# The opening of an attention and two-layer expert kernel: a new order of loads, sums, Newton's chain and weight conversions

## The chip, the cores and the metric

The kernel runs on one core of one Trainium2 chip. The core has TensorE (matrix products and transposes, PE in the profile, its weight loads PEld), VectorE (DVE), ScalarE (ACT), GpSimd (POOL) and SyncE (SP), whose queue issues the transfers between device memory and on-chip memory here. The metric is the time of one execution in microseconds (us) on the device, as a median of several runs.

## The reference, cut to what matters

First comes Nystrom attention over 4 batches of 8 heads, 576 rows and 64 columns per head. The rows are averaged in 32 groups of 18 to landmarks, and an inverse is found by Newton's iteration. Then two gated layers of 2304 tokens follow, 512 wide and 1536 inside.

```
m = 32; scale = 1.0 / np.sqrt(D)
q_lm = q.reshape(B, H, m, S // m, D).mean(axis=3)
k_lm = k.reshape(B, H, m, S // m, D).mean(axis=3)
A, Bm, C = sm(q, k_lm), sm(q_lm, k_lm), sm(q_lm, k)      # sm: softmax of scale * a @ b.T
Z = Bm.T / (norm1(Bm) * norminf(Bm) + 1e-06)
for _ in range(6):
    Z = 2 * Z - Z @ Bm @ Z
x = (A @ Z @ C @ v)                                      # heads side by side: 2304 x 512
x = (silu(x @ w_gate) * (x @ w_val)) @ w_out
out = (sigmoid(x @ w2_gate) * (x @ w2_val)) @ w2_out
```

## The kernel before, in words

A batch `b` is worked on in two groups `g` of four heads; the four heads' 32 landmarks each fill the 128 partitions. The steps of attention are generators:

- `front(b, g)`, word `F`: `lm_steps` for the key, then for the query. The 18 rows of each landmark are summed (`lm`): VectorE does it in one reduction for group (0,0), POOL by halving additions (L127 to L132) for all others. TensorE transposes the sum (`lt`), ScalarE makes the block-diagonal `bdk` or `bdq` from it, and nine transposes `tp` with ScalarE copies make `kq` (kT or qT). Then `cs`, the scores of the landmark queries against all keys, VectorE's maximum `cmx`, ScalarE's exponential `e`; the small matrix `bm` with its exponential `bs` and `rc`, a reciprocal; transposes of `e` (`et`), and the product with v (`cv`, scaled into `bc`, BC in the code). Last come the scores of all queries (`as`) with `amx`, the subtraction and exponential (`sx`).
- `back(b)`, word `B`: `bs` of both groups is divided by its sums, `rr` is made from its largest row and column sums, and Newton's chain runs on the pair [small matrix, C v] side by side (`nw` on TensorE, `rw` on VectorE, five turns and one last that gives UU), then `ut`, the transposed result. `a_steps` normalizes `sx`, transposes it and splits it into a high and a low half (`AH`, two per group); one step of it is given after each Newton turn by `step(ga)`.
- The first layer's weights (`c` is one of six chunks of 256 inner columns) come in as `raw` tiles, three buffers, four transfers of 128 KB each for the four tiles of a chunk, and are converted to float32 words (`convert`: two ScalarE instructions, L329 and L332, two of VectorE, L334 and L338). `wo` tiles, two buffers, hold the output weights. These steps are `wfill`.
- Word `U` (`uw_steps`): the product of `ut` and the converted weights (`pu`), split into two halves `uw`; it starts with a two-column product (`pu<-ident`) that needs neither. Word `G` (`gv1_steps`): gate and value products `pg`, `pv` of `AH` and `uw`. Both need both groups' `AH` and `uw`. Word `O`: the output product `po`. `I` and `J` give conversion steps until a chunk's inputs or outputs are ready.

The words of `first` are given in order, L812 on. A planner lays out each engine's queue from that: it estimates when an instruction can start and prefers what was given first, so the order in a queue is not quite the program's. At run time each queue goes in order. A tile asked for under a tag takes one of its buffers and waits until the readers of the old one are done. All transfers named here go through SP's queue; a transfer that waits for a buffer holds back those behind it. `load_next` asks for a group's input two groups ahead (v one ahead), into four buffers `in` and one `vin`.

The lines that the prediction speaks of: L120 to L152 (landmarks), L157 to L224 (rest of `front`), L226 to L242 (`AH`), L251 to L305 (`back`), L309 (first loads), L318 to L341 (`convert`), L346 (`load_in`), L812 (order).

## Time and profile before

| | us |
|---|---|
| median of 3 runs (867.75 to 869.99) | 869.67 |
| the profiled execution | 868.88 |
| its span, first to last instruction | 867.1 |
| TensorE busy in the span | 839.1 (97%) |
| VectorE busy | 660.2 (76%) |
| ScalarE busy | 474.2 (55%) |
| POOL busy | 58.5 (7%) |

The span in 40 equal slices of 21.7 us, busy share in tenths, with the granted TensorE clock and the DMA engines' share:

```profile
PE   6698999999999999999999999999999999999998
...
DVE  4989886866976987579698667879778985578655
ACT  5687565455752754237257655555647385455431
...
PEclk9899999999999999999999999999999999999999
DMA  8776311022520631006114316244335552232003
```

A digit is a mean over its slice. TensorE is below 9 in the first, second and fourth slice, and its clock in the second. The opening of the attention lies in these slices, up to 87 us; from there on TensorE's digits are 9 up to the last.

### The profile page before, as it was taken

The page shows a single profiled execution, that of the slowest core. Times are in us where ns is not written, and L with a number is a line of the kernel's source. Part 1 is how long each engine was busy: PE and PEld are TensorE (multiplying, and loading weights), DVE is VectorE, ACT ScalarE, POOL GpSimd, SP SyncE. Part 2 cuts the span into 40 slices and gives each one's busy share as a digit, 9 for nine tenths or more (in the row PEclk, how much of TensorE's full clock was granted, in tenths as well). Part 3 has the DMA queues.
Part 4 walks back from the last instruction along what each step waited for, and adds up shares of the span by engine and source line. Part 5 has one row for each costly group of instructions (what it writes and reads, how often), then busy time and mean ns, then how long its engine had stood idle before and what let it go on. Part 6 is the DMA issues. An engine that isn't in the chain of part 4 may idle for free.

```text
span 867.1 us, 15869 instructions
## 1 busy us (share of the span) xinstructions
PE 839.1 (97%) x6172; PEld 695.4 (80%) x6172; DVE 660.2 (76%) x1295; ACT 474.2 (55%) x967; POOL 58.5 (7%) x90
## 2 busy tenths in 40 slices
PE   6698999999999999999999999999999999999998
PEld 4476778898788888888878888888888888888886
DVE  4989886866976987579698667879778985578655
ACT  5687565455752754237257655555647385455431
POOL 4644330000000000000000000000000000000000
PEclk9899999999999999999999999999999999999999
DMA  8776311022520631006114316244335552232003
GB/s 261 200 222 199 110 56 30 2 77 55 161 98 2 195 98 50 1 25 220 49 43 152 122 41 203 87 157 142 125 126 170 166 176 97 68 122 73 5 20 97
DMA packets 41483, 93.31 MB, mean 108 GB/s; under 512 B 5824, under 2 KB 8896, under 8 KB 41408
## 3 DMA queue, kind: packets, MB, share of 16 engines
q1 hardware_dynamic: 40256, 90.72, 33.2%
q10 hardware_dynamic: 1152, 1.57, 0.8%
q8 instruction: 48, 0.79, 0.4%
q14 instruction: 27, 0.22, 0.1%
HBM read 72.88 MB, written 19.40 MB: 106 GB/s over the span
## 4 chain that ended last, share of the span: by engine, by line
PE 87%; DVE 6%; ACT 3%; DMA 2%; issue 1%; SPq 0%; ACTq 0%; DVEq 0%
PE po L65 33%; PE pg L65 21%; PE pv L65 21%; PE pu L65 3%; PE pgr L65 2%; PE pvr L65 2%; DMA raw<-in_moe_w_val_dram 1%; PE tp L148 1%; PE nw L65 1%; PE cs L65 1%; PE as L65 1%; DVE xl L366 1%; ACT cv L329 1%; PE et L198 1%; DVE lm L134 0%
## 5 line engine op out<-in xcount | busy, mean ns | idle before, releaser
L65 PE MATMUL po<-wo,h 128*128 128x512 f32 x432 | 109.9, 391 | 0.0
L65 PEld LDWEIGHTS po<-h,wo 128*128 128x128 f32 x480 | 82.6, 188 | 27.8 <-issue 5.9
L65 PE MATMUL po<-h,wo 128*128 128x512 f32 (+1 forms) x480 | 104.3, 373 | 0.0
L65 PE MATMUL pg<-AH,uw 128*128 128x288 f32 x552 | 94.8, 299 | 1.3 <-ACT uw L365 1.0
L65 PEld LDWEIGHTS po<-wo,h 128*128 128x128 f32 x432 | 80.7, 188 | 17.6
L65 PE MATMUL pv<-AH,uw 128*128 128x288 f32 x552 | 91.7, 296 | 0.5 <-DVE sg L537 0.5
L772 DVE TENSOR_TENSOR oacc<-po,oacc 128x512 f32<-128x512 f32 x90 | 60.0, 682 | 36.2 <-PE po L65 36.1
L65 PEld LDWEIGHTS pg<-AH,uw 128*128 128x128 f32 x552 | 80.1, 188 | 6.4 <-issue 2.5
L65 PEld LDWEIGHTS pv<-AH,uw 128*128 128x128 f32 x552 | 78.9, 188 | 4.0 <-issue 1.7
L329 ACT ACTIVATE cv<-raw 128x512 f32<-128x512 f32 x84 | 56.8, 677 | 31.8 <-DVE st L338 8.9
L334 DVE SCALAR_TENSOR_TENSOR cv<-cv,cv 128x512 uint32<-128x512 uint32 x84 | 57.8, 690 | 1.8 <-ACT cv L332 1.6
L65 PE MATMUL po<-hh,wo 128*128 128x288 f32 x256 | 58.9, 310 | 0.0
L332 ACT ACTIVATE cv<-raw 128x512 uint32<-128x512 uint32 x84 | 55.9, 670 | 2.1 <-DVE wo L366 2.1
L595 DVE TENSOR_TENSOR acc<-po,acc 128x512 f32<-128x512 f32 x64 | 43.3, 685 | 15.6 <-PE po L65 15.4
L540 ACT ACTIVATE sg<-pg 128x288 f32<-128x288 f32 x64 | 26.0, 407 | 46.7 <-PE pg L65 46.4
L65 PE MATMUL pg<-AH,wk 128*128 128x512 f32 x192 | 50.0, 390 | 0.0
L65 PE MATMUL pv<-AH,wk 128*128 128x512 f32 x192 | 49.5, 389 | 0.0
L65 PEld LDWEIGHTS po<-hh,wo 128*128 128x128 f32 x256 | 41.6, 189 | 4.8 <-issue 2.4
L365 ACT CAST h<-h 128x288 fp32r<-128x288 f32 x64 | 27.5, 431 | 29.9 <-DVE h L541 29.9
L366 DVE TENSOR_TENSOR h<-h,h 128x288 fp32r<-128x288 f32 x64 | 29.1, 456 | 17.9 <-ACT h L365 17.6
L65 PEld LDWEIGHTS pv<-AH,wk 128*128 128x128 f32 x192 | 36.0, 188 | 7.5
L65 PEld LDWEIGHTS pg<-AH,wk 128*128 128x128 f32 x192 | 35.7, 188 | 7.4 <-ACT c5g L694 0.2
(206 smaller groups left out, 1759.7 us busy)
## 6 DMA issues: line engine op xcount, KB each, us to landing
raw<-in_moe_w_out_dram SPq DMA_DIRECT2D x36, 512.0 KB, 3.9
raw<-in_moe_w_gate_dram SPq DMA_DIRECT2D x48, 128.0 KB, 3.4
raw<-in_moe_w_val_dram SPq DMA_DIRECT2D x48, 128.0 KB, 3.4
raw<-in_moe_w_gate_dram SPq DMA_DIRECT2D x24, 256.0 KB, 3.0
raw<-in_moe_w_val_dram SPq DMA_DIRECT2D x24, 256.0 KB, 3.7
wkd<-st SPq DMA_DIRECT2D x24, 256.0 KB, 3.2
wtd<-tf SPq DMA_DIRECT2D x12, 512.0 KB, 3.3
st<-wkd SPq DMA_DIRECT2D x24, 256.0 KB, 3.5
```

The lines of the kernel that those rows point to most:

```text
L65: return nc.tensor.matmul(o, l, r, start=start, stop=stop, skip_group_check=True)
L148: nc.tensor.transpose(ps[:, j], flat(src[:, 2 * u:2 * u + 2]), ident)
L198: nc.tensor.transpose(ps[:, j, :], flat(e[:, r // 2, r % 2]), ident)
L329: nc.scalar.activation(t0, hiw.bitcast(F32), AF.Copy, scale=2.0 ** -112)
L332: nc.scalar.activation(u1, low, AF.Copy, scale=0.875 * 2.0 ** -29, bias=0.49)
L334: nc.vector.scalar_tensor_tensor(u1, u0, 3, u1, op0=ALU.logical_shift_left, op1=ALU.bitwise_or)
L365: nc.scalar.copy(hi, x)
L366: nc.vector.tensor_tensor(lo, x, hi.bitcast(F32), op=ALU.subtract)
L540: nc.scalar.activation(sg, pss[0], AF.Silu)
L595: nc.vector.tensor_tensor(sl, ps, sl, op=ALU.add)
L772: nc.vector.tensor_tensor(acc, ps, acc, op=ALU.add)
```

## The change

The first loads are given as k, q of group (0,0), k, q of group (0,1), v(0,0), the first raw weight tile, v(0,1). Two of these tiles stand in `wo` buffers: v(0,1), and the fourth raw tile of chunk 0. The second raw tile is given behind the issue of k(1,0), the third and fourth behind q(1,0). `lm` has two buffers. The key of group (0,1) is summed by VectorE as the first group is, its copy made by VectorE, and its `bdk` has a buffer of its own. In `back`, `bs` is scaled per group, and ScalarE makes `BC` from the unscaled `bs` with the scale as its operand. For batch 0, the steps of `front(0,0)`, `front(0,1)` and `back(0)` are given by hand: up to Newton's end first, then the first weights' conversions, then `as`, `sx` and `a_steps`. `tc.issue_after(x)` puts every instruction given inside the block behind x in x's own engine's queue: one conversion behind `bs` (ScalarE) and `rc` (VectorE) of group (0,0), three behind `BC` and `rr`; the rest of group (0,0) up to `cv` behind the query transpose `lt` of group (0,1) on TensorE.

```diff
     inq = {}
+    mark = {}
     def load_attn(b, which, g):
         if which == "v":
-            t = att.tile([TP, 4, R, D], F32, tag="vin", name=f"vin{b}_{g}", bufs=1)
-            nc.sync.dma_start(t, v[b, 4 * g:4 * g + 4].rearrange("h (p r) d -> p h r d", r=R))
+
+            pool_, tag, bufs = (per, "wo", 2) if (b, g) == (0, 1) else (att, "vin", 1)
+            t = pool_.tile([TP, 4, R, D], F32, tag=tag, name=f"vin{b}_{g}", bufs=bufs)
+            ins = nc.sync.dma_start(t, v[b, 4 * g:4 * g + 4].rearrange("h (p r) d -> p h r d", r=R))
         else:
             t = att.tile([P, L, D], F32, tag="in", name=f"{which}in{b}_{g}", bufs=4)
             src = {"q": q, "k": k}[which]
-            nc.sync.dma_start(t, src[b, 4 * g:4 * g + 4].rearrange("h (t u) d -> (h t) u d", u=L))
+            ins = nc.sync.dma_start(t, src[b, 4 * g:4 * g + 4].rearrange("h (t u) d -> (h t) u d", u=L))
         inq[which, b, g] = t
+        mark[which, b, g] = ins.ins
     NU = L // 2
...
     def load_next(b, g, which):
         i = AORDER.index((b, g)) + (1 if which == "v" else 2)
-        if i < len(AORDER):
+        if i < len(AORDER) and (which, *AORDER[i]) not in inq:
             load_attn(AORDER[i][0], which, AORDER[i][1])
     def step(fill, n=1):
...
         def lm_steps(which):
             src = inq[which, b, g]
-            lm = sm("lm", [P, 2, D], 1)
-
-            if (b, g) > (0, 0):
+            lm = sm("lm", [P, 2, D])
+
+            if (b, g, which) not in ((0, 0, "k"), (0, 0, "q"), (0, 1, "k")):
                 x = sm("ls", [P, NU, D], 1)
                 nc.gpsimd.tensor_tensor(x, src[:, 0:NU], src[:, NU:], op=ALU.add)
                 nc.gpsimd.tensor_tensor(x[:, 0:4], x[:, 0:4], x[:, 4:8], op=ALU.add)
...
                     nc.gpsimd.tensor_tensor(lm[:, w], x[:, 0], x[:, 1], op=ALU.add)
             else:
                 nc.vector.tensor_reduce(lm[:, 0], src.rearrange("p u d -> p d u"), axis=AX.X, op=ALU.add)
-                nc.scalar.copy(lm[:, 1], lm[:, 0])
+                (nc.vector.tensor_copy if g else nc.scalar.copy)(lm[:, 1], lm[:, 0])
             yield
             ps = pst(b, [P, P], "lt", g)
-            nc.tensor.transpose(ps, flat(lm), ident)
-            bdt = sm("bd" + which, [P, 2, P], 1)
+            mark["lt", which, b, g] = nc.tensor.transpose(ps, flat(lm), ident).ins
+
+            bdt = (per.tile([P, 2, P], F32, tag="CL", name="bdk01", bufs=16) if (b, g, which) == (0, 1, "k") else
+                   sm("bd" + which, [P, 2, P], 1))
             for w in range(2):
                 nc.scalar.activation(bdt[:, w], ps, AF.Copy, scale=pmask[:, w:w + 1])
             yield
...
             mm(ps[hs], bdq[:, 0, hs], bdk[:, 0, hs])
         nc.vector.tensor_reduce(bmx, ps, axis=AX.X, op=ALU.max)
         nc.vector.tensor_scalar(bs[:, g], ps, bmx, None, op0=ALU.subtract)
-        nc.scalar.activation(bs[:, g], bs[:, g], AF.Exp, scale=8.0, accum_out=bsm[:, g:g + 1])
+        mark["bs", b, g] = nc.scalar.activation(bs[:, g], bs[:, g], AF.Exp, scale=8.0, accum_out=bsm[:, g:g + 1]).ins
         rc = sm("rc", [P, 1])
         nc.vector.tensor_scalar(rc, csm[:, 0:1], csm[:, 1:2], 1e-9, op0=ALU.add, op1=ALU.add)
-        nc.vector.reciprocal(rc, rc)
+        mark["rc", b, g] = nc.vector.reciprocal(rc, rc).ins
         yield
         eT = sm("eT", [TP, R, P], 1)
         for hf in range(2):
...
         for g in range(2):
             nc.vector.tensor_scalar(bsm[:, g:g + 1], bsm[:, g:g + 1], 1e-9, None, op0=ALU.add)
         nc.vector.reciprocal(bsm, bsm)
-        nc.vector.tensor_tensor(bs, bs, bsm[:, :, None].to_broadcast([P, 2, M]), op=ALU.mult)
-        nc.scalar.copy(BC[:, :, 0:M], bs)
-
-        bmt = sm("bmt", [P, 2, M])
+        for g in range(2):
+            mark["BC", b] = nc.scalar.activation(BC[:, g, 0:M], bs[:, g], AF.Copy, scale=bsm[:, g:g + 1]).ins
+            nc.vector.tensor_scalar(bs[:, g], bs[:, g], bsm[:, g:g + 1], None, op0=ALU.mult)
+
+        nb = sm("nb", [P, 4, M], 1)
+        bmt = nb[:, 0:2]
         nc.vector.transpose(out=flat(bmt), in_=flat(bs))
         nrm = sm("nrm", [P, 2, 2])
         nc.vector.tensor_reduce(nrm[:, 0], bs, axis=AX.X, op=ALU.add)
         nc.vector.tensor_reduce(nrm[:, 1], bmt, axis=AX.X, op=ALU.add)
         yield
-        nb = sm("nb", [P, 4, M], 1)
         nc.vector.tensor_copy(nb, nrm.rearrange("p a b -> p (a b)")[:, :, None].to_broadcast([P, 4, M]))
         nbt = sm("nbt", [P, 4, M], 1)
         nc.vector.transpose(out=flat(nbt), in_=flat(nb))
...
         for g in range(2):
             nc.vector.tensor_scalar(rr[:, g:g + 1], nmax[:, 0, g:g + 1], nmax[:, 1, g:g + 1], 1e-6,
                                     op0=ALU.mult, op1=ALU.add)
-        nc.vector.reciprocal(rr, rr)
+        mark["rr", b] = nc.vector.reciprocal(rr, rr).ins
         yield
...
             RW2 = sm("rw", [P, 2, 96], 2)
             nc.vector.scalar_tensor_tensor(RW2, RW, 2.0, ps, op0=ALU.mult, op1=ALU.subtract)
             RW = RW2
-            step(ga)
+            if b:
+                step(ga)
             yield
         ps = prod(RW)
         UU = flat(sm("rw", [P, 2, 96], 2))[:, 0:P].rearrange("p (g d) -> p g d", g=2)
...
         while ga:
             step(ga)
             yield
-
-    for g in range(2):
-        for x in "kqv" if g == 0 else "kq":
-            load_attn(0, x, g)
     W1 = {}
...
         return per.tile([P, 2, 2 * FC], U32, tag="raw", name="raw", bufs=3)
     def load_in(layer, c, kk):
-        t = raw_tile()
+
+        t = raw_tile() if (layer, c, kk) != (0, 0, 3) else per.tile([P, 2, 2 * FC], U32, tag="wo", name="raw3", bufs=2)
         for j, w in enumerate(((wg1, wv1), (wg2, wv2))[layer]):
             if layer == 0:
...
     KINDS = {"F": front, "B": back, "I": lambda c: weights_to(c, 3), "J": lambda c: weights_to(c, 5),
              "U": uw_steps, "P": uw_steps, "G": gv1_steps, "O": o1_steps}
+    def advance(gen, n):
+        for _ in range(n):
+            next(gen, None)
+
     def emit(word, nw=1):
         gens = [iter(KINDS[t[0]](*map(int, t[1:]))) for t in word.split("+")]
         fill = word[0] in "UPGO"
...
             if fill:
                 step(wfill, nw)
+
+    for g, x in ((0, "k"), (0, "q"), (1, "k"), (1, "q"), (0, "v")):
+        load_attn(0, x, g)
+    load_to(1)
+    load_attn(0, "v", 1)
     wfill.extend(weights(0, c) for c in range(2))
     first = (
-        "F00 F01 B0 I0 F10 U00 G00 F11 J0 O00 B1 I1 U10 G10 J1 F20 O10 U01 G01 "
+        "I0 F10 U00 G00 F11 J0 O00 B1 I1 U10 G10 J1 F20 O10 U01 G01 "
         "F21 U11 B2+F30 O01 G11 F31 U02 O11 G02 B3 U12 O02 G12 U03 O12 G03 U13 O03 G13"
     )
+
+    f0, f1, b0 = front(0, 0), front(0, 1), back(0)
+    advance(f0, 14)
+    with tc.issue_after(mark["k", 1, 0]):
+        load_to(2)
+    with tc.issue_after(mark["q", 1, 0]):
+        load_to(4)
+    advance(f1, 10)
+    with tc.issue_after(mark["lt", "q", 0, 1]):
+        advance(f0, 3)
+    advance(f1, 7)
+    advance(b0, 10)
+    with tc.issue_after(mark["bs", 0, 0]), tc.issue_after(mark["rc", 0, 0]):
+        step(wfill, 3)
+    with tc.issue_after(mark["BC", 0]), tc.issue_after(mark["rr", 0]):
+        step(wfill, 9)
+    for gen in (f0, f1, b0):
+        advance(gen, 99)
     for w in first.split():
         emit(w)
     wfill.append(weights(0, 2))
```

## Rows read from the trace of the kernel before

**Rows 1.** The page, part 4: the chain that ended last, by engine.

```profile
PE 87%; DVE 6%; ACT 3%; DMA 2%; issue 1%; SPq 0%; ACTq 0%; DVEq 0%
```

**Rows 2.** Windows: length, busy time (instructions) of PE, PEld, DVE, ACT, POOL; PEclk, DMA share, GB/s.

```profile
4.76:24.55 19.79, 14.75 (x237) 11.09 (x238) 11.50 (x28) 12.23 (x38) 11.37 (x19) 1.00 0.93 280
24.55:41.73 17.18, 13.29 (x256) 7.92 (x254) 16.15 (x38) 11.75 (x26) 11.46 (x16) 0.86 0.71 188
41.73:50.00 8.27, 6.19 (x154) 3.92 (x155) 7.94 (x20) 7.63 (x18) 0.00 (x0) 0.67 0.70 215
...
50.00:70.00 20.00, 19.83 (x261) 17.34 (x261) 16.57 (x46) 16.67 (x44) 9.15 (x12) 1.00 0.81 229
70.00:90.00 20.00, 16.92 (x211) 11.91 (x211) 19.05 (x41) 13.90 (x33) 9.46 (x12) 1.00 0.66 186
90.00:110.00 20.00, 19.58 (x273) 15.93 (x272) 15.57 (x38) 9.68 (x27) 7.45 (x12) 1.00 0.27 87
```

**Rows 3.** Timeline of VectorE: start us, length, instruction, [idle before <-releaser].

```profile
...
7.74 2.13 DVE L134 TENSOR_REDUCE lm<-qin 128x64 f32<-128x1152 f32 x1 [0.91 <-PE lt L138]
...
13.38 0.94 DVE L170 TENSOR_REDUCE cmx<-cs 128x1 f32<-128x288 f32 x2 [3.51 <-PE cs L65]
...
23.96 0.21 DVE L190 TENSOR_SCALAR rc<-csm 128x1 f32<-128x1 f32 x1
...
24.55 1.21 DVE L254 TENSOR_TENSOR bs<-bs,bsm 128x64 f32<-128x64 f32 x1
...
29.82 0.32 DVE L288 TENSOR_TENSOR rw<-nw,rr 128x192 f32<-128x192 f32 x1
...
40.59 0.27 DVE L299 SCALAR_TENSOR_TENSOR rw<-rw,nw 128x128 f32<-128x128 f32 x1
...
```

**Rows 4.** Timeline of TensorE.

```profile
...
20.56 0.69 PE L65 MATMUL cs<-kq,bdq 128*32 128x288 f32 x8
...
39.46 0.53 PE L65 MATMUL nw<-rw 32*32 32x96 f32 x16 [0.99 <-DVE rw L293]
...
43.35 1.96 PE L65 MATMUL pu<-w,ut 64*32 64x512 f32 x16 [1.95 <-DVE w L338]
...
49.86 0.40 PE L65 MATMUL pg<-AH,uw 128*128 128x288 f32 x1
...
```

**Rows 5.** Timeline of POOL.

```profile
...
10.27 1.40 POOL L127 TENSOR_TENSOR ls<-kin 128x576 f32<-128x576 f32 x1 [8.97 <-DMA kin<-in_k_dram]
...
24.27 1.41 POOL L127 TENSOR_TENSOR ls<-qin 128x576 f32<-128x576 f32 x1
...
```

**Rows 6.** SP's timeline, then the DMA issues of v and q(0,1) with us to landing.

```profile
1.66 0.42 SPq L74 DMA_DIRECT2D vin<-in_v_dram  x1
...
2.83 0.45 SPq L78 DMA_DIRECT2D qin<-in_q_dram  x1
...
vin<-in_v_dram SPq DMA_DIRECT2D x1, 576.0 KB, 7.4
...
qin<-in_q_dram SPq DMA_DIRECT2D x1, 576.0 KB, 9.5
```

**Rows 7.** L254's source view (ns min/median/max), then VectorE groups up to 90 us.

```profile
L254 DVE TENSOR_TENSOR bs<-bs,bsm x4: 224/225/1211, 24.6 to 154.5; 128x64 f32<-128x64 f32 x4
...
L338 DVE SCALAR_TENSOR_TENSOR w<-cv,cv 128x512 uint32<-128x512 uint32 x8 | 6.1, 762 | 0.0
...
L221 DVE TENSOR_TENSOR sx<-as,amx 128x320 f32<-128x320 f32 (+1 forms) x8 | 3.5, 453 | 0.1
...
L220 DVE TENSOR_REDUCE amx<-as 128x10 f32<-128x320 f32 (+1 forms) x8 | 3.5, 448 | 0.0
...
L233 DVE TENSOR_TENSOR sx<-sx,asm 128x576 f32<-128x576 f32 x4 | 3.4, 841 | 0.0
...
L239 DVE TENSOR_TENSOR AH<-sx_0t,AH 128x576 fp32r<-128x576 f32 x2 | 2.3, 1166 | 0.1
...
```

**Rows 8.** The chain of waits, 0 to 130 us: start, length, what.

```profile
...
61.62 5.48 DMA raw<-in_moe_w_val_dram
...
```

## The prediction

> **What bounds the kernel now.** The page's chain that ended last comes first: TensorE carries 87% of it [rows 1], so time is lost only where TensorE idles or its clock is down. The windows show where [rows 2]: between 4.76 and 90 us TensorE is idle for 5.04 + 3.89 + 2.08 + 0.17 + 3.08 = 14.26 us (length less PE column), and the granted clock is 0.86 and 0.67 of full in the second and third stretch, so partly at the lower of its two levels, 1.2 GHz. VectorE's column beside it is idle for 8.29 us up to 24.55, and then only for 1.03, 0.33, 3.43 and 0.95 up to 90. So the opening has two halves: up to 24.55 a chain of landings, sums and handovers sets the pace; after it VectorE is nearly full, and TensorE waits for it.
>
> The VectorE timeline shows the first half [rows 3]: the first query's sum waits 0.91 us for the transpose of the first key's (`lm` has one buffer), the first maximum waits 3.51 us, and `rc` of the second group comes at 23.96. TensorE's timeline beside it [rows 4] has the second group's scores at 20.56, though POOL began that key's sum on landing, at 10.27 [rows 5]. Then comes Newton's chain: `rw` at 29.82, five turns to 40.59 [rows 3]; `pu` at 43.35, released by the last conversion of the first weights, and steady `pg` at 49.86 [rows 4].
>
> **The change part by part.**
>
> *Loads.* v is issued at 1.66 and takes 7.4 us to landing, q(0,1) at 2.83 and 9.5 [rows 6]: landings at 9.1 and 12.3, with the key at 10.2 between. Given last, v leaves these three places to k, q and v: k at 9.1, q at 10.2, v at 12.3. The first tile's four issues and v(0,1) follow, none with a buffer to wait for; v(0,1), 1.1 MB later at the 280 GB/s of this stretch [rows 2], lands at 16, ahead of its product (19 to 20). Twelve more weight issues of about 0.6 us now stand in SP's queue behind k(1,0) and q(1,0), which wait for their buffers, and ahead of k(1,1): that comes some 5 us later, for a group whose scores run after `pg` starts. I price this at nothing; cover gone, k(1,1) holds F11 back by those 5 us. The slots lent by `wo` come free with the product and the fourth conversion, before 33, where the first `wo` tile is written: nothing.
>
> *Sums.* The second `lm` buffer takes the 0.91 us out: the query's sum runs 6.85 to 8.98, and the first group comes 0.9 sooner. VectorE's sum of the second key starts at 9.1 and takes 2.13 as the query's does [rows 3], its copy 0.2: done at 11.4, inside the 3.51 us wait. It costs VectorE 2.3 us of work and the path nothing. POOL starts the second query at 10.2 and needs the 3.8 us that the key took there (10.27 to 14.09): 14.0. With `bdk` of its own, the second group's scores can start at 15.0 instead of 20.56 [rows 4]. ScalarE shortens this lead: it is busy for 12.23 us of 4.76 to 24.55 [rows 2], gets one conversion of 1.3 more and loses 0.9 of exponentials, so even dense it ends past 18. I take `rc` at 19.5 instead of 23.96, 4.5 us; the bounds are 0.9 (the buffer alone) and 5.6 (the scores' full lead).
>
> *Normalizing.* One product of 1.21 us at 24.55 [rows 3] becomes two scalings of half its width. The same product takes 0.22 in the median of its four [rows 7], so two take 0.24 each at most if undisturbed. But a scaling writes `bs` where ScalarE's `BC` has yet to read it, so the first waits for a ScalarE instruction, some 0.35 with its handover: 0.85 in all, a gain of 0.35. The long one lies beside POOL's addition from 24.27 to 25.68 [rows 5] and ends at 25.76; if the new ones meet such an addition, or `BC` stands behind a 1.3 us pair of ScalarE, it is a loss of up to 1. What is queued on VectorE behind that wait is the whole of `rr`; on ScalarE behind `BC`, the held conversions, for which nobody waits before 33. Batches 1 to 3 pay some 0.25 us of VectorE each, under full TensorE: nothing. `bmt` inside `nb` adds a dependency within VectorE's own order: nothing. Between 27.16 and 29.14 the trace has five VectorE instructions of the second group's scores among those that make `rr`; they now stand behind Newton, 1.4 us. So `rw` starts at 19.5 + (29.82 - 23.96) - 0.35 - 1.4 = 23.6.
>
> The Trainium skill, "SBUF — State Buffer", section "Who interferes with whom", says that a VectorE instruction with two SBUF inputs blocks against a GpSimd one that reads SBUF, and that `tensor_scalar` in a two-port mode can take the same lock. For the old product the trace agrees (1.21 us beside POOL's 1.41); for the new form it would take the 0.35 away and put the end as much later.
>
> *Newton first.* Six turns lie between 29.82 and 40.59, 1.80 each [rows 3], with one to three other VectorE instructions in each. Bare, a turn is 0.53 of `nw` matmuls [rows 4], 0.34 of VectorE and two handovers of 0.06: 1.0. Now six instructions of the three held conversions, 0.76 each [rows 7], fill the gaps. I take 1.35, nearer the bare one, since one of them nearly fits beside the 0.53; 1.0 and 1.8 are the bounds. UU comes at 23.6 + 8.1 = 31.7 and `ut` 1.2 later, as before, at 32.9. The conversions need 4.5 us of VectorE and 4.0 of ScalarE after 23 and end there too. `pu` can start at 33.4 instead of 43.35.
>
> *What is late next.* `pg` needs `AH` of both groups. For each that is two maxima and two subtractions of the scores (0.45 each), a sum of 0.74, two short ones of 0.45 together, the product of 0.84, the transpose of 0.76 and the subtraction of 1.17 or 0.85 [rows 7]: 5.6, for both 11.2 us of VectorE. This work was stepped through Newton's turns and now stands behind them. I count 5 us of holes for it between 13 and 33, so 6.2 are left; F10's VectorE work, some 4.3, and the split's 1.3 are in the same queue. Steady `pg` comes at 33.4 + 6.2 + 4.3 + 1.3 = 45.2 instead of 49.86, 4.7 us.
>
> *What of it reaches the end.* VectorE is full again in 70 to 90, idle 0.95, where TensorE is idle 3.08 [rows 2], so I go by VectorE's ledger. Of its 8.29 idle us up to 24.55 there stay the wait for the key (0.3), for the first scores (1.1), for the exponentials (1.3) and some 1.7 of handovers, 4.4; saved 3.9. Added work is 2.3 less 0.73 (1.21 for 0.48), 1.6: net 2.3. Of its 3.43 in 50 to 70, where the chain waits 5.48 us for a weight tile [rows 8], I take near half, 1.5: that tile's buffer comes free some 8 us sooner. Sum 2.3 + 1.5 = 3.8. The profiled execution took 868.88 (span 867.1 and 1.8 around it), 0.8 less than the median of 869.67. The forecast is 865.1 from the one and 865.9 from the other: 865.4.
>
> **The rivals.** *The whole lead is carried.* TensorE has 19.8 us of work in 50 to 70, and VectorE 4.4 us free in 90 to 110 for the backlog [rows 2]. Then 8 of the 14.26 idle us go: 861. Against it stands the full VectorE in 70 to 90.
>
> *VectorE takes it back, or the planner does.* The scores and `AH`, given last, fill fewer holes than I count; or the planner leaves the second group's transposes behind the first group's work, and the scores stay near 20. Then the buffer's 0.9 and the 0.35 are left: 868.
>
> *Slower: `AH` becomes the last wait.* If none of its 11.2 us is done before `ut`, and F10 (4.3) and the first `wo` conversions (two of 1.5, two subtractions of 0.7: 4.4) go ahead of it, steady `pg` comes at 32.9 + 11.2 + 4.3 + 4.4 = 52.8, 2.9 us after 49.86: 872. It decides when less than 2.9 us of `AH` gets into the holes. For it: VectorE is idle for only 1.03 us between 24.55 and 41.73 [rows 2]. Against it: the holes before 24.55 stay half open, and the scores' inputs are there early.
>
> **How the numbers follow.** Forecast 0.50 (its own range 863 to 867), whole lead 0.14, taken back 0.23, slower 0.13. About 0.3%, 2.6 us, is what a measurement of this kernel can tell from no change. Faster by more has the first two, 0.64; within has the third, 0.23; slower the last, 0.13. The range 860.5 to 870.0 holds the forecast, most of the whole lead and of the third case, and leaves out the last.
>
> **What would show it.** Right: the query's sum at 6.85, the second key's on VectorE at about 9.1, second scores at 15, `rw` at 23 to 24, turns of 1.0 to 1.5 us, `pu` near 33, steady `pg` near 45, VectorE idle for about 4 us up to 20. Wrong: second scores after 18 (the planner), turns of 1.8 (conversions in the chain), `pu` early but `pg` near 50 (`AH`), or an idle TensorE in 60 to 90 that grows by what the opening gained.

## The result, and the profile after

The changed kernel takes 873.95 us (median of 6 runs, 872.72 to 876.69); the kernel before, run beside it, 868.84 (6 runs). The ratio is 1.0065 [1.0051, 1.0079]: slower by 5 us, where 865.4 was forecast. The profiled execution of the changed kernel took 876.69, the longest of its six, with a span of 874.9. Its traces are read for where things happen; sizes are taken from the medians.

First the windows [rows 2], same columns.

```profile
4.76:24.55 19.79, 14.93 (x245) 10.70 (x248) 12.05 (x26) 13.75 (x44) 9.89 (x14) 1.00 1.01 294
24.55:41.73 17.18, 12.03 (x240) 8.07 (x232) 12.75 (x31) 8.06 (x19) 11.23 (x18) 0.80 0.89 271
41.73:50.00 8.27, 4.75 (x45) 2.12 (x40) 8.01 (x19) 3.89 (x8) 1.67 (x3) 0.68 0.05 16
50.00:70.00 20.00, 18.81 (x233) 15.04 (x232) 17.70 (x38) 15.28 (x41) 5.68 (x9) 0.88 0.47 126
70.00:90.00 20.00, 18.14 (x289) 12.44 (x293) 17.21 (x45) 15.18 (x39) 8.15 (x12) 1.00 0.68 193
90.00:110.00 20.00, 19.18 (x309) 16.45 (x298) 17.78 (x47) 10.83 (x28) 6.88 (x9) 1.00 0.49 150
```

VectorE (third busy column) is idle for 7.74 us up to 24.55, where it was idle for 8.29 and was to be idle for 4.4, though 2.36 us of what it does there is new work (the second key's sum and its copy). In the second stretch it is idle for 4.43 instead of 1.03. TensorE idles 16.58 us up to 90 instead of 14.26. From 100 us on everything in this execution is late by about the same 7.7 us to the end (`pg` at 103 and at 435 us, the span by 7.8), so the loss is made before. Over the first two windows VectorE did 24.80 us of work instead of 27.65.

VectorE's timeline shows how [rows 3].

```profile
6.54 2.11 DVE L138 TENSOR_REDUCE lm<-qin 128x64 f32<-128x1152 f32 x1
8.57 2.16 DVE L138 TENSOR_REDUCE lm<-kin 128x64 f32<-128x1152 f32 x1
...
15.03 0.21 DVE L196 TENSOR_SCALAR rc<-csm 128x1 f32<-128x1 f32 x1 [1.57 <-ACT e L181]
...
18.64 0.46 DVE L176 TENSOR_REDUCE cmx<-cs 128x1 f32<-128x288 f32 x1 [3.17 <-PE cs L65]
...
21.90 0.21 DVE L196 TENSOR_SCALAR rc<-csm 128x1 f32<-128x1 f32 x1 [0.55 <-ACT e L181]
...
23.70 0.87 DVE L262 TENSOR_SCALAR bs<-bs,bsm 128x32 f32<-128x32 f32 x2 [1.23 <-ACT bc L261]
...
25.18 0.48 DVE L226 TENSOR_REDUCE amx<-as 128x10 f32<-128x320 f32 x1
...
28.02 1.71 DVE L338 SCALAR_TENSOR_TENSOR cv<-cv,cv 128x512 uint32<-128x512 uint32 x1
29.66 0.34 DVE L295 TENSOR_TENSOR rw<-nw,rr 128x192 f32<-128x192 f32 x1
...
35.23 0.35 DVE L300 SCALAR_TENSOR_TENSOR rw<-rw,nw 128x192 f32<-128x192 f32 x1 [3.50 <-PE nw L65]
...
44.23 0.29 DVE L307 SCALAR_TENSOR_TENSOR rw<-rw,nw 128x128 f32<-128x128 f32 x1
...
50.06 0.76 DVE L245 TENSOR_TENSOR AH<-sx_1t,AH 128x576 fp32r<-128x576 f32 x1 [0.21 <-ACT AH L244]
```

The sums come as forecast (6.54, 8.57). Then the holes stay empty: 1.57 us before `rc`, 3.17 before the second scores' maximum, 0.55 and 1.23 behind them. In the kernel before, the first group's score work (`amx` to the product on `sx`) stood between 18.3 and 24.0; here its first instruction is the `amx` at 25.18. Up to 33 us VectorE did 2.2 us of both groups' score and `AH` work, where it had done 8.2. The second `rc` leads by 2.06 us (21.90 for 23.96), and `rw` comes at 29.66, where it came at 29.82: the lead is gone before Newton's chain begins. UU comes at 44.23 instead of 40.59, and the last `AH` at 50.06.

TensorE's timeline [rows 4]:

```profile
16.48 0.67 PE L65 MATMUL cs<-kq,bdq 128*32 128x288 f32 x2
...
27.93 0.42 PE L65 MATMUL as<-bdk,kq 128*32 128x64 f32 x14
32.53 0.80 PE L65 MATMUL as<-bdk,kq 128*32 128x64 f32 x18 [4.18 <-issue]
...
45.45 1.96 PE L65 MATMUL pu<-w,ut 64*32 64x512 f32 x16 [0.52 <-DVE ut L311]
48.45 0.61 PE L65 MATMUL pg<-AH,uw 128*128 128x288 f32 x1 [1.04 <-ACT uw L370]
...
57.54 0.40 PE L65 MATMUL pg<-AH,uw 128*128 128x288 f32 x1
...
59.24 1.06 PE L65 MATMUL pg<-AH,uw 128*128 128x288 f32 x6
```

Between 28.35 and 32.53 TensorE stands still for nothing that the trace names ("issue"), in the middle of a row of like matmuls. The DMA view of 28 to 33 us shows what shared the transfers' time (queue: packets, MB, share; then one group of issues with the us to landing; mean 304 GB/s):

```profile
q8 instruction: 1, 0.02, 1.6%
...
raw<-in_moe_w_gate_dram SPq DMA_DIRECT2D x2, 128.0 KB, 7.6
```

Queue q8 (instruction) is taken to bring TensorE's program; e1 below tests that. The page's table of queues has (packets, MB, share)

```profile
q8 instruction: 48, 0.79, 0.4%
```

so 16 KB a packet, and its chain that ended last [rows 1] now has 2% of issue:

```profile
PE 88%; DVE 7%; ACT 2%; issue 2%; DMA 1%; SPq 0%; ACTq 0%; DVEq 0%
```

In the trace's packet records the one of this stretch runs from 29.78 to 31.10, and TensorE goes on 1.4 us after it. In the kernel before, packets of q8 came at 24.58 and 30.83, and TensorE did not stop for them. Behind the stall TensorE's granted clock is at the lower of its two levels, 1.2 GHz:

```profile
33.00:36.00 3.00, 3.00 (x34) 2.03 (x25) 0.77 (x2) 1.35 (x4) 2.69 (x5) 0.50 1.03 255
```

### The profile page after: what moved, and what is told of

Read it like the earlier page. It is cut to its first block, busy times and chain, and to the rows that moved or that the text cites. A ratio compares the mean times of both kernels' runs of the same rounds, so it can differ in the third digit from the quotient of the medians.

```text
span 874.9 us, 15866 instructions
## 1 busy us (share of the span) xinstructions
PE 843.8 (96%) x6172; PEld 698.0 (80%) x6172; DVE 662.9 (76%) x1301; ACT 473.4 (54%) x971; POOL 53.3 (6%) x84
## 3 DMA queue, kind: packets, MB, share of 16 engines
q10 hardware_dynamic: 1152, 1.57, 0.8%
## 4 chain that ended last, share of the span: by engine, by line
PE 88%; DVE 7%; ACT 2%; issue 2%; DMA 1%; SPq 0%; ACTq 0%; DVEq 0%
PE po L65 33%; PE pg L65 21%; PE pv L65 21%; PE pu L65 3%; PE pgr L65 2%; PE pvr L65 2%; PE tp L154 1%; PE nw L65 1%; PE as L65 1%; PE cs L65 1%; PE cv L65 1%; PE et L204 1%; DVE xl L371 1%; DVE lm L138 0%; DVE cv L338 0%
## 5 line engine op out<-in xcount | busy, mean ns | idle before, releaser
L65 PE MATMUL pg<-AH,uw 128*128 128x288 f32 x552 | 97.1, 302 | 3.4 <-ACT uw L370 2.3
L65 PE MATMUL pv<-AH,uw 128*128 128x288 f32 x552 | 93.8, 299 | 1.0 <-DVE sg L542 0.9
```

Of the source, the lines that this page charges most:

```text
L65: return nc.tensor.matmul(o, l, r, start=start, stop=stop, skip_group_check=True)
```

## The experiments

The letters in the quoted texts. **A**: TensorE's program came late behind 1.8 MB of attention loads, and the stall is the loss. **B**: the stall belongs to the instruction that it stands before. **C**: the order gives the score work and `AH` too late, so that they are waited for last; **D** is C made sharper: VectorE carries the opening, holes left empty can't be had back, and VectorE's work is what counts. Ratios are to the kernel before, run on the same chip beside each.

| kernel | median us | ratio |
|---|---|---|
| e1_pad32 | 882.88 | 1.0159 [1.0146, 1.0173] |
| e2_hold | 872.93 | 1.0048 [1.0032, 1.0064] |
| e3_ah_in_newton | 878.44 | 1.0098 [1.0080, 1.0116] |
| e4_bc_back | 875.18 | 1.0062 [1.0049, 1.0075] |
| e5_as_early | 870.03 | 1.0014 [1.0001, 1.0026] |
| e6_as_hold | 874.29 | 1.0053 [1.0032, 1.0073] |
| e7_loads | 869.86 | 1.0006 [0.9991, 1.0022] |
| e8_loads_sum | 870.01 | 1.0015 [1.0002, 1.0029] |
| e9_order | 878.48 | 1.0110 [1.0090, 1.0129] |
| e10_pool_key | 872.25 | 1.0032 [1.0019, 1.0046] |
| e11_nohold | 872.62 | 1.0042 [1.0026, 1.0058] |
| e12_lm2 | 868.78 | 0.9995 [0.9983, 1.0007] |
| e13_hold2 | 873.59 | 1.0057 [1.0044, 1.0071] |
| e14_order_early | 876.49 | 1.0084 [1.0061, 1.0107] |
| e15_hold2_early | 869.67 | 1.0007 [0.9996, 1.0017] |
| e16_nohold_early | 871.17 | 1.0023 [1.0013, 1.0033] |

### What the stall is, and what it is worth

**e1_pad32**: 32 small products ahead of TensorE's program.

```diff
+    pad = ptile([P, 2], "n", "pad")
+    for _ in range(32):
+        mm(pad, ident, ident[:, 0:2])
```

> The changed kernel with 32 two-column products in front of everything on TensorE, while it waits for the first key (0.7 to 7 us). They add 64 rows (weight load and product) to TensorE's program. In the changed kernel TensorE stands still for 4.2 us at 28.35, after its 705th row, with nothing shown that it waits for; a transfer of 16 KB on the instruction queue moves at 29.8 to 31.1, and TensorE goes on 1.4 us later. Theory A, the stall is TensorE's program arriving late behind the data transfers: it belongs to a place in the count of rows, so here it comes again after row 705 (plus or minus 5), 64 rows earlier in the program, where `as` of the first group stands. Theory B, it is a dependence of that instruction that the profile doesn't show: it comes at the same `as` instruction, after row 769. Time by A: 872 to 876, the stall being of another length at another place; by B the same as the changed kernel, 874.

The pads took 13.8 us, far more than meant, so the time says nothing. But they shift the program by 127 rows in the trace (matmuls, weight loads and the semaphore events among them counted together), and the gap shows what the stall follows: it stands after row 705 in the changed kernel and again after row 705 here, before another instruction, 2.55 us long, with the packet at 35.27 to 36.52. The stall follows the place in the program, not the instruction: B falls. Queue q8 has 49 packets here instead of 48, as a longer program would. Gaps after row 705 in e3, e4 and e9 agree (2.98, 2.02 and 0.72 us): in all five TensorE goes on 1.4 to 1.7 us after a packet's end.

**e2_hold**: k(1,1), q(1,1) and v(1,0) are issued behind chunk 1's first raw tile. **e13_hold2** holds only q(1,1) and v(1,0), **e15_hold2_early** is e13 with the first group's scores given early (next part).

```diff
...
-            load_attn(AORDER[i][0], which, AORDER[i][1])
+            if AORDER[i] == (1, 1) and which != "v" or (which, *AORDER[i]) == ("v", 1, 0):
+                held.append((AORDER[i][0], which, AORDER[i][1]))
+            else:
+                load_attn(AORDER[i][0], which, AORDER[i][1])
...
+    load_to(7)
+    with tc.issue_after(mark["raw", 1, 0]):
+        for x in held:
+            load_attn(*x)
```

> The changed kernel with three loads of 0.59 MB (k and q of group (1,1), v of group (1,0)) issued in SP's queue behind the first weight tile of chunk 1, some 8 us later, instead of at 23.4 to 24.9. The instruction transfer that came at 29.8 then has 1.8 MB less in front of it. Theory A (program late behind transfers): the 4.2 us stall of TensorE shrinks below 1 us, Newton's first turn moves from 34.3 to about 30.3, and the kernel takes 870 (gain of 3 to 4). Theory C, the stall only covers other late work (`AH` given last, weights of chunk 1 late): the stall may go, but steady `pg` stays near 57 and the time within 1.5 us of 874. By theory B nothing changes.

> The changed kernel with q(1,1) and v(1,0) alone behind the first raw tile of chunk 1, k(1,1) where it was: 1.15 MB less stands ahead of the second packet of TensorE's program, which should come near 26 instead of 29.78, with no gap after row 705. If the stall is the loss (theory A), first pg and the end come 3 to 4 us sooner, 870. If the empty holes are the loss (theory D), Newton's chain comes sooner but G00 does not, 873 to 874, with VectorE's busy time up to 24.55 still under 12.5 us.

> The run with the early scores (870.03) and the two loads held: no stall in either, so the difference is the price of holding the loads by itself. 870 if it is free; the run that held all three and gave the scores early took 874.29, so up to 873 if holding is what cost there.

In both e2 and e13 the packet comes sooner (26.55 and 26.88) and the gap after row 705 is gone. TensorE's timeline of e13:

```profile
30.11 0.66 PE L158 MATMUL tp<-ident,kin 128*128 128x128 f32 x4
30.70 0.53 PE L65 MATMUL nw<-rw 32*32 32x96 f32 x16
...
41.34 1.09 PE L65 MATMUL pu<-w,ut 64*32 64x512 f32 x16 [1.08 <-DVE ut L315]
43.21 0.40 PE L65 MATMUL pg<-AH,uw 128*128 128x288 f32 x1 [0.78 <-ACT uw L374]
...
45.44 0.85 PE L65 MATMUL pg<-AH,uw 128*128 128x288 f32 x3 [1.56 <-DVE uw L375]
...
54.75 1.04 PE L65 MATMUL pg<-AH,uw 128*128 128x288 f32 x6
```

`pu` is 4.1 us sooner than in the changed kernel, and 2.0 sooner than in the kernel before; the first `pg` comes at 43.21. Yet runs of six `pg` begin only at 54.75, and the median is 873.59 for 873.95. The stall was real, and it was late program, but by the ratios taking it away is worth 0.7 us (e13: 1.0057 for 1.0065) or 1.5 (e2), both within the intervals: A does not explain the 5 us. Holding two loads costs nothing that can be measured: e15 takes 869.67; e5, the same without the hold, 870.03 (its packet comes at 24.30, and it has no stall either). And e13 and e15 differ only in where the first group's scores are given, neither has the stall, and 3.9 us lie between them, on one chip. So where the scores are given costs most of the 5 us, without A. It is the place in the order that this shows; that the way from there to the end is VectorE's work, as D has it, rests on the ledger below.

**e4_bc_back**: the old product of `bs` and the old copy to `BC`.

```diff
-        for g in range(2):
-            mark["BC", b] = nc.scalar.activation(BC[:, g, 0:M], bs[:, g], AF.Copy, scale=bsm[:, g:g + 1]).ins
-            nc.vector.tensor_scalar(bs[:, g], bs[:, g], bsm[:, g:g + 1], None, op0=ALU.mult)
+        nc.vector.tensor_tensor(bs, bs, bsm[:, :, None].to_broadcast([P, 2, M]), op=ALU.mult)
+        mark["BC", b] = nc.scalar.copy(BC[:, :, 0:M], bs).ins
```

> The changed kernel with `bs` divided by one product on VectorE and `BC` copied after it, as in the kernel before. In the changed kernel the two scalings wait 1.23 us for ScalarE's `BC`, which stands behind two `eT` copies. If that wait counts, `rr` comes about 0.5 to 1 us earlier, or no earlier if the product meets a POOL addition again (1.21 us). With the stall of TensorE behind it, which ends at 32.5 whatever `rr` does, the time should not move: 873 to 875 by theories A and C; 873 if this wait were the cause of a part of the loss.

No difference that can be measured, with 2.02 us of the stall still there: the 1.23 us wait for `BC` isn't what costs.

### Where the score work is given

**e5_as_early** gives the rest of `front(0,0)`, its scores, ahead of the second group's last seven steps; **e6_as_hold** is that with e2's hold, **e14_order_early** and **e16_nohold_early** are that in e9 and e11 (next part); **e3_ah_in_newton** gives both groups' scores behind `advance(f1, 7)`, ahead of `back`, and one step of `AH` after each Newton turn.

```diff
     advance(f1, 10)
     with tc.issue_after(mark["lt", "q", 0, 1]):
         advance(f0, 3)
+    advance(f0, 99)
     advance(f1, 7)
```

> The changed kernel, with the first group's scores of all queries, their maxima, subtractions and exponentials given ahead of the second group's last seven steps, so that they can fill VectorE's holes of 3.17 us (18.64) and 1.15 to 1.57 us (before 15). Theory D (VectorE's ledger: work that was given behind Newton's chain left holes empty that cannot be had back) expects VectorE busier by about 2 us up to 24.55 (12.7 instead of 10.70), first pg some 1.5 to 2 us earlier and 872 us. Theory A (the loss is TensorE's program that arrives late behind the weights' transfers, after row 705) expects the same gap after row 705 and 874, no change, because the packet's time is not touched. A third outcome, slower than 874, would say that the scores push the second group's small scores back.

> The same early scores, and the three attention loads k(1,1), q(1,1), v(1,0) behind the first raw tile of chunk 1 (as in the run that held these loads, 872.93). If both costs are real and add up (A about 1 us as measured, D about 2 us), 870 to 871; if the VectorE ledger is all, the same as the run with the early scores alone, 872; if holding the loads makes VectorE idle later, over 873.

> The changed kernel with the scores' and `AH`'s work of batch 0 given ahead of Newton's chain and stepped through its turns, as in the kernel before; loads, sums, normalizing and held conversions stay. If giving `AH` last is what costs (theory C): `AH` of both groups is done before `ut`, steady `pg` comes 3 to 5 us earlier than in the changed kernel, and the time is 870 to 871. If the stall alone costs (theory A): the stall of about 4 us is still there, as the transfers are the same, and the time stays at 873 to 875.

e5 gets back 4 of the 5 us; the stall is gone in it too, so e13 against e15 is the cleaner pair. VectorE's timeline of e15, whose order there is that of e5, shows the hole before the second maximum partly filled: scores at 19.21, the second group's first maximum at 21.30, where it stood at 18.64 in the changed kernel.

```profile
19.21 0.49 DVE L230 TENSOR_REDUCE amx<-as 128x10 f32<-128x320 f32 x1 [2.65 <-PE as L65]
19.73 0.49 DVE L231 TENSOR_TENSOR sx<-as,amx 128x320 f32<-128x320 f32 x1
...
20.96 0.41 DVE L230 TENSOR_REDUCE amx<-as 128x8 f32<-128x256 f32 x1
21.30 0.44 DVE L180 TENSOR_REDUCE cmx<-cs 128x1 f32<-128x288 f32 x1
...
31.53 0.36 DVE L299 TENSOR_TENSOR rw<-nw,rr 128x192 f32<-128x192 f32 x1
```

So `rw` comes 1.3 us later than in e13 (30.21), and the kernel is 3.9 us faster: the start of Newton's chain isn't what the end hangs on. e3 is slower than the changed kernel, where C expected a gain: it gives the second group's scores early as well, ahead of `rr`, and its stall (2.98 us after row 705) stays. It tells that more ahead of Newton isn't better by itself. e6 (874.29) missed too: the early scores should have helped e2, and it stands 4 us by the ratios above e15, which differs from it only in letting k(1,1) go early. Why k(1,1)'s place costs that here, and nothing between e2 and e13, stays open; TensorE's clock was lower in e6 (below).

### The parts of the change alone

**e7_loads** has the new loads and buffers, with the rest as before; **e8_loads_sum** has VectorE's sum of the second key too (all but the order by hand, the holds and the new normalizing); **e9_order** has the order by hand and the holds of conversions and of `lt` alone (old loads, buffers, POOL's sum of the second key and old normalizing); **e12_lm2** only the second `lm` buffer, for which `bmt` stands inside `nb` as in the change; **e10_pool_key** is e5 with the second key summed by POOL; **e11_nohold** is the changed kernel without holds on the conversions. In turn: what e8 changes in the changed kernel (beside the lines of e4), what e9 changes there (likewise, beside the `lm` and `bdk` buffers, the key's sum and the two tiles in `wo`), what e10 changes in e5 and e7 in e8, what e11 changes in the changed kernel, and e12 in the kernel before:

```diff
-            if b:
-                step(ga)
+            step(ga)
...
-        "I0 F10 U00 G00 F11 J0 O00 B1 I1 U10 G10 J1 F20 O10 U01 G01 "
+        "F00 F01 B0 I0 F10 U00 G00 F11 J0 O00 B1 I1 U10 G10 J1 F20 O10 U01 G01 "
...
-    f0, f1, b0 = front(0, 0), front(0, 1), back(0)
-    advance(f0, 14)
...
-    for gen in (f0, f1, b0):
-        advance(gen, 99)
```

```diff
...
-    for g, x in ((0, "k"), (0, "q"), (1, "k"), (1, "q"), (0, "v")):
+    for g, x in ((0, "k"), (0, "q"), (0, "v"), (1, "k"), (1, "q")):
         load_attn(0, x, g)
-    load_to(1)
-    load_attn(0, "v", 1)
...
-    with tc.issue_after(mark["k", 1, 0]):
-        load_to(2)
-    with tc.issue_after(mark["q", 1, 0]):
-        load_to(4)
```

```diff
-            if (b, g, which) not in ((0, 0, "k"), (0, 0, "q"), (0, 1, "k")):
+            if (b, g, which) not in ((0, 0, "k"), (0, 0, "q")):
```

```diff
-    with tc.issue_after(mark["bs", 0, 0]), tc.issue_after(mark["rc", 0, 0]):
-        step(wfill, 3)
-    with tc.issue_after(mark["BC", 0]), tc.issue_after(mark["rr", 0]):
-        step(wfill, 9)
+    step(wfill, 12)
```

```diff
-            lm = sm("lm", [P, 2, D], 1)
+            lm = sm("lm", [P, 2, D])
...
```

> The new loads and buffers alone (v last, twelve weight issues behind k(1,0) and q(1,0), two lm buffers), with POOL's sum of the second key, the old normalizing and the order of before. If the 2.3 us that the second key's sum adds to VectorE are what the run with loads and sum paid (870.0), this gives 868 to 868.5, no difference from before. If the loads are what it paid, 870 again.

> The new loads, buffers and VectorE's sum of the second key, but the order of before (the words F00 F01 B0, one step of AH after each Newton turn, nothing held) and the old normalizing. Theory D (the order by hand is what costs) expects 867 to 869: no loss left, and perhaps the gain of the sum that the prediction counted. If the loads or the sum are the cause (the packets of the program late behind the weights' transfers, the 2.3 us added to VectorE), 872 to 874, with a gap of over 1 us in TensorE's rows where a packet is late.

> The other half alone: the old loads, buffers, POOL's sum of the second key and the old normalizing, with the order by hand (Newton first, conversions held, AH after Newton). Theory D expects 871 to 874: the order alone brings the loss, since the second scores stay near 20 and VectorE's work is given later. If loads and sum are the cause, 868 to 870.

> The kernel before with two lm buffers and nothing else (the two small tiles nb and bmt share their room, as in the change). The 0.91 us wait of the second sum goes, and the first group comes 0.9 us sooner. If the whole lead were carried: 867.6. By the ledger (VectorE full after 24.55, half of it lost in other waits): 868 to 868.5, within what can be measured.

> The run with the early scores (870.03), but POOL sums the second key. By the VectorE ledger 2.36 us of VectorE's work go, but the second key's sum ends near 12.5 instead of 10.7: 868 to 869.5 if the hole before the second scores is covered by the early scores, 872 or more if the second group's scores are what Newton's chain waits for.

> The changed kernel without holding the twelve conversion steps (they are given at the same place, and the planner may put them anywhere). Theory D: conversions then fill some of VectorE's holes before 20 and none stands between rr and rw, but the scores are still given last: 871 to 873. If the holds cost nothing, 874 as the changed kernel. If the planner puts conversions ahead of the exponentials of the second group, over 875.

> The order alone (old loads, POOL's sum of the second key, old normalizing: 878.48, the worst of all, with a stall of only 0.72 us), with the first group's scores given ahead of the second group's last seven steps. Theory D: VectorE's 4.12 us hole before the second scores takes some 3 us of them, and most of the 9 us comes back: 870 to 874. Theory A: there is no stall to take away, 877 to 878.

> The changed kernel with the early scores and without the holds on the conversions. The holds cost 1.3 us with the scores late (872.62 against 873.95). Theory D: the scores now fill the holes, the conversions follow as in the old order: 869 to 870, no better than before, since VectorE still has the second key's 2.36 us more to do. If the rest of the loss in the run with early scores is the holds, 868.5 or less.

The loads cost and bring nothing that can be measured, the buffer neither; loads and sum together are at most a little slower. The order by hand alone loses nearly 10 us, with only a 0.72 us stall. Its first window and VectorE's hole:

```profile
4.76:24.55 19.79, 13.11 (x154) 9.07 (x158) 7.11 (x14) 10.70 (x31) 13.15 (x22) 1.00 0.78 246
```

```profile
20.80 0.46 DVE L175 TENSOR_REDUCE cmx<-cs 128x1 f32<-128x288 f32 x1 [4.12 <-PE cs L65]
```

VectorE does 7.11 us of work there instead of 11.50 [rows 2]: with POOL's slower sum the second scores start at 19.00 (20.56 in the kernel before), and the order leaves nothing to do ahead of them. The loads and the sum hide half of this in the changed kernel. With early scores the order alone gets back only 2 us (e14), not the 4.5 or more that D named: there the scores push the second maximum from 20.80 to 24.71. What of the remaining 7 is the hold behind `lt` and what the held conversions wasn't tried apart. e10 hints that the sum is worth its work under the order by hand: without it e5's ratio goes from 1.0014 to 1.0032 (the intervals overlap). The holds of the conversions may cost some 2 us in the changed kernel (e11: 1.0042 for 1.0065, the intervals just overlap), and nothing that can be measured once the scores are early (e16: 1.0023 for e5's 1.0014).

### The ledger over the traces

I counted VectorE's work started by 50 us, each instruction at the undisturbed duration of its form (the 20th percentile of that operation and shape over these traces), less 2.3 us where it sums the second key, and set it beside the first `pg` and the span of the profiled execution, all against the kernel before (37.5 us of work, `pg` at 47.0, span 867.1). The last column is the time by the ratio.

| trace | VectorE's work by 50 | first `pg` | span | by the ratio |
|---|---|---|---|---|
| changed kernel | -6.2 | +1.5 | +7.8 | +5.6 |
| e9_order | -5.7 | +3.4 | +9.2 | +9.6 |
| e10_pool_key | -3.2 | -0.1 | +2.6 | +2.8 |
| e13_hold2 | -2.7 | -3.7 | +3.8 | +5.0 |
| e15_hold2_early | -1.1 | -3.5 | +1.1 | +0.6 |
| e5_as_early | -0.7 | -2.4 | -0.3 | +1.2 |
| e8_loads_sum | +1.1 | -1.9 | -0.3 | +1.3 |

The first `pg` says little about the end: in e13 it is 3.7 us early, and the end is 3.8 us late. The work that VectorE still owes says more. The traces not shown lie likewise, save e6 (-2.0 and +6.1); e1, whose work starts 8 us late, is left out. It is a correlation of single executions, and by itself shows no cause. By the ratio it is looser: from the changed kernel to e13 the owed work falls by 3.5 us and the time by 0.7, from e13 to e15 by 1.6 and the time by 4.3. So how the work left undone reaches the end is argued, not shown.

The ledger leaves TensorE's clock out. Length times what the granted clock lacks of full speed sums to 8.5 us over the changed kernel's six windows and to 5.1 over those of the kernel before. That alone doesn't part these kernels. Executions with a mean granted clock of 0.994 took 872.72 to 874.41 in the changed kernel and 868.00 to 870.34 in the kernel before (13 of those beside the experiments); at 0.998 e13 took 872.72 and e15 868.98 to 869.77. For e6 it may: its executions have 0.990 to 0.992 and e15's 0.994 to 0.998, so no two can be compared at one clock.

## Why the prediction was wrong

- **What bounds the kernel**: right as far as the runs tell. With VectorE's entries as measured, its ledger gives a loss, as came out. The forecast failed in the entries.
- **Loads**: right. e7 prices them at nothing. Not foreseen was that the dense transfers also delay TensorE's program; by e13 and e2 that is 0.7 to 1.5 us of the loss, which can't be told from none.
- **Sums**: the sums ran as worked out (query at 6.54, key at 8.57), the second scores began at 16.48 instead of 15.0, but `rc` came at 21.90 instead of 19.5: 2.06 us of lead where 4.5 were taken, inside the bounds of 0.9 and 5.6. TensorE had the first group's `et` and `cv` among the scores (17.09 to 18.9), so their second half was done at 19.4, 2.9 us after the first began where it had taken 1.3 (20.56 to 21.8), and its maximum, behind a conversion, began at 19.80. The three `kq` copies ahead of the exponential on ScalarE cost nothing: it starts 0.34 us after `nmx`, as in the kernel before (22.37 to 22.70). VectorE's `nmx`, then ScalarE's timeline:

```profile
20.29 0.21 DVE L179 TENSOR_SCALAR nmx<-cmx 128x1 f32<-128x1 f32 x1
...
19.52 1.24 ACT L155 COPY kq<-tp 128x384 f32<-128x384 f32 x3 [1.20 <-PE bm L65]
20.63 0.68 ACT L181 ACTIVATE e<-cs,nmx 128x288 f32<-128x288 f32 x1
...
22.59 0.85 ACT L205 COPY eT<-et 96x384 f32<-96x384 f32 x2 [0.51 <-PE et L204]
23.34 0.54 ACT L261 ACTIVATE bc<-bs,bsm 128x32 f32<-128x32 f32 x2
```

- **Normalizing**: wrong, and it took the rest of the lead. `BC` stood behind the two `eT` copies above, the wait was 1.23 instead of 0.35, the two scalings took 0.87 instead of 0.48, and no room was won behind `rr`: the planner put five other score instructions there, at 25.18 to 27.55, four of the first group and one of the second. (Of the five that the prediction took out, one, `bc` at 27.16, is no score work: Newton's chain needs it.) A conversion of 1.71 us stands between `rr` and `rw`. From `rc` to `rw` it took 7.76 us (29.66 - 21.90) instead of 5.86 [rows 3] where 4.1 were forecast (23.6 - 19.5). The possible loss of up to 1 us was named, not taken. Those two scalings are a place for the Trainium skill, "SBUF — State Buffer", section "Who interferes with whom": `tensor_scalar` can, in a two-port mode, be blocked by GpSimd at the pair of ports that the two share. In e15, where no POOL instruction runs beside them, they took 0.24 and 0.23; in the changed kernel, with one from 23.77 to 24.52, 0.24 and 0.66, the second ending at 24.57. The traces agree.
- **Newton first**: six turns took 14.57 us (29.66 to 44.23). The first, with 2.87 us of the stall in it, took 5.57 (to 35.23), the other five 1.80 each for the 1.35 taken, at the bound of 1.8. Without the stall e13 has 1.56 over its six, inside 1.0 and 1.8.
- **What is late next**: this is the step that failed. "I count 5 us of holes for it between 13 and 33": not one score instruction of the first group ran before 25.18, since they were given behind `back`, and the planner prefers what was given first. The holes were there, 6.5 us of them, and held nothing; of the score and `AH` work VectorE had done 2.2 us by 33, between `rr`'s instructions, where 5 were counted. e13 against e15 puts the place of these scores at 3.9 us. Steady `pg` came at 57.5, past the 52.8 of the rival.
- **What reaches the end**: the ledger had VectorE's idle time at 4.4 us up to 24.55, saved 3.9; it was 7.74, saved 0.55, against added work of 2.36. The second stretch, which the sum left as it was, had 3.4 us more of idle time, 3.50 us in one piece behind TensorE's stall (35.23). The 1.5 us of 50 to 70 came out near, idle 2.30 for 3.43, but 70 to 90 took them back: idle 2.79 for 0.95.
- **The rivals**: "Slower: `AH` becomes the last wait" came closest, at 872 for 873.95, but not by its path. Its sign, less than 2.9 us of that work in the holes, was met with none. Yet 6.8 us of the work ran ahead of `ut` (45.11), where it has none, and the last `AH` ended at 50.82, 6.7 us before steady `pg`, so `AH` was not the last wait; between them TensorE ran F10's `et`, `cv` and `as` among `pg` in ones and twos. That the time fits is in part luck. Its chance of 0.13 was set against holes that "stay half open", without asking which instruction the order would put into them.

None of the sixteen beats the kernel before. e12, e7 and e15 can't be told from it: two that leave its order alone, and one in which the scores are early and no packet is late.

## What to carry to other kernels

When one engine carries a stage, an order by hand that lets the critical chain go first must also say what fills that engine's holes; look at which instructions the new order makes available at each hole, and don't count the hole as used. Milestones of the chain (`pu` and the first `pg` in e13) can come earlier and the end later: in these traces the undone work of the full engine was the better sign. A lead of a few us needs every step from its start to its use followed in the queue of the engine that makes it: here `et` and `cv` on TensorE among the scores, and the `eT` copies on ScalarE ahead of `BC`.

## What the runs showed of the hardware that was not expected

- TensorE's program comes in 16 KB packets over the same DMA engines as the data. Where 1.8 MB of loads had been issued just ahead (23.43 to 24.52) and the DMA engines' share was 0.91 and more, a packet came late and TensorE stood still 4.18 us, after row 705 of the trace; with two of the three loads held (e13), the packet came 2.9 us sooner and there was no stall. The Trainium skill, "Runtime: NRT & Kernel Launch", section "Instruction fetch mechanics", has the 16 KiB blocks and calls their cost mostly hidden; these traces show gaps of 2.0 to 4.2 us after row 705 in the changed kernel, e1, e3 and e4, and of 0.72 in e9.
- A conversion of 0.68 us took 1.71 (28.02) beside POOL's first addition, 1.64 in e15 (22.09) and 1.77 in e13 (19.54), each beside one of the 1.40 us additions:

```profile
27.77 1.41 POOL L131 TENSOR_TENSOR ls<-kin 128x576 f32<-128x576 f32 x1 [1.65 <-DMA kin<-in_k_dram]
```

- The 32 products of two columns at the start of e1 took 13.8 us, 0.43 each (two rows apiece in the trace).
